# First block in a fixed program order, second norm's scale and shift moved behind the transpose, w1/w3 loaded in 4-chunk pieces

## The chip, the cores and the metric

The kernel runs on one core of a Trainium2 chip. The core has five engines that work side by side, each through its own instructions in order: PE (TensorE, matrix multiplies and transposes, writing to PSUM), DVE (VectorE, elementwise work), ACT (ScalarE, elementwise functions and PSUM copies), POOL (GpSimd) and SP (SyncE, which here issues nearly all DMA loads and stores). The metric is the device time of one execution in microseconds (us), lower is better; several runs are made and the median is given.

## What is computed

One transformer-like block over a sequence of S=2048 rows of D=576 values: a conditioned layer norm, a long convolution over the sequence, a gate, a residual, a second conditioned layer norm and a gated feed-forward layer of width F=4608. In short:

```python
sa, ca, ga, sb, cb, gb = split(silu(c) @ w_mod, 6)          # six rows of 576
h  = layernorm(x) * (1 + ca) + sa
ks = sum over t of k shifted by (3 - t) * shift_k[:, 3 - t]  # 4 taps
kv = ks * v
y  = irfft2(rfft2(kv padded) * rfft2(ssm_k padded))[:S] + kv * ssm_D
x  = x + ga * (h * y)
h  = layernorm(x) * (1 + cb) + sb
x  = x + gb * ((silu(h @ w1) * (h @ w3)) @ w2)
```

All inputs are bfloat16. w1 and w3 are 576 x 4608, w2 is 4608 x 576, w_mod is 576 x 3456.

## The kernel before

**Tiling.** The sequence is cut into 8 blocks of 256 rows and 4 rounds of 512 rows (two blocks each). The feed-forward part of a round r runs in two stages. `hidden` computes 128 columns of F at a time (a chunk; there are 36): 16 full matmuls and 2 pairs' worth of half-height ones (L512, L520) into PSUM, a Silu and a copy on ACT (L526, L528) and a product on DVE (L529) into `h3`. `down` then multiplies `h3` by w2 in 288 matmuls of 288 columns (L551); its results go through DVE (`og`, L559, L560) to the output.

**Convolution.** A block s is prepared by `kv_block` (4 taps times k, times v: eight DVE operations of 1152 elements, L252 to L258; then a forward transform on PE, L236, with PSUM copies on ACT, L239, giving `X`), `k_block` (transposes of ssm_k, L278, and a transform giving `W` and `V`), `pair` (products of one X with one V, 3456 elements each, L316, summed into `z`, L318), `gate` (layer norm of x, scaled and shifted by `arow` and `brow`) and `finish`: real parts of z (L377, L378), the inverse transform on PE (L387, 16 matmuls), times the gate (`ty`, L391) and added to x (L393), statistics on ACT (L335, L337) and POOL (L342 to L346), the second norm on DVE (L358 centers, L360 scales by the row `cbrow`, L361 shifts by `sbrow`, L417 repeats the last 64 columns), ten transposes on PE (L406) and two copies on ACT (L408) into `h2T`, which is what `hidden` of the next round reads. X and V of old blocks are stored to and read back from DRAM (`Xd`, `Vd`).

**What sets the order.** The convolution of round r+1 is written as a generator. `advance` is called after each chunk of `hidden` and each four chunks of `down` and takes as many steps out of the generator as `rate` times the cost of that piece of work allows; each `yield` says what its step cost. `rate` is the generator's total divided by a time that the round is thought to take. `end()` takes whatever is left after the last matmul of `down`. The instructions so written are then put in order on each engine by a scheduler that has its own idea of their durations. After that the order on an engine is fixed: an instruction that waits holds up all behind it on its engine, and that holds for SP's DMA issues too.

**Start.** `early_loads` issues on SP: ssm_k block 0 (`knat`), k block 0 (`kh`), v, x, and the six column groups of w_mod; on ACT's queue c, D and shift_k. shift_k is loaded to all 128 partitions at once (576 KB). `cond` makes silu(c), `mod_piece(m)` one row of 576 on all partitions with ten matmuls (L171). Round 0's `hidden` runs its first N1=20 chunks twice: once for block 0 alone (256 columns wide, while block 1's convolution, `conv_second`, is worked out), and later for block 1.

**Weights.** `load_w13` brings a piece of FC=2 chunks of w1 and w3 (four DMAs: two of 256 KB in rows of 512 B, two of 32 KB, L487, L488) into one of NW13=3 buffers `wst`. A buffer is loaded again when the matmuls that read it are done.

```python
    def advance(self, cost):
        self.due += cost
        while self.due > 0 and self.steps is not None:
            c = next(self.steps, None)
...
            self.due -= c
```

Of the kernel before, what the change touches and what calls it, by code (L numbers as in the profile page):

```python
# [10 lines left out]
F32 = mybir.dt.float32  # L11
# [14 lines left out]
FC = 2  # L26
NW13 = 3
W2C = 4
NW2 = 4
N1 = 20  # L30
# [9 lines left out]
class _Kernel:  # L40
# [28 lines left out]
    def setup(self):  # L69
# [17 lines left out]
        self.cbrow = const.tile([P, D], BF16, name="cbrow")  # L87
        self.sbrow = const.tile([P, D], BF16, name="sbrow")
# [13 lines left out]
        nc.vector.memset(self.neghalf[:], -0.5)  # L102
        nc.gpsimd.memset(self.knat[64:P, 4, :], 0.0)
        make_identity(nc, self.ident[:])

    def early_loads(self):
        nc = self.nc
        self.crow = self.hp.tile([1, D], BF16, name="crow", tag="sg")
        self.load_k(0)
        nc.scalar.dma_start(self.crow[:], self.c)  # L110
        nc.scalar.dma_start(self.drow[:], self.ssm_D.rearrange("(o d) -> o d", o=1))
        self.shk_raw = self.prod.tile([P, D, 4], BF16, name="shk_raw", tag="p")
        bap = bass.AP(tensor=self.shift_k.tensor, offset=self.shift_k.offset,
                      ap=[[0, P], [4, D], [1, 4]])
        nc.scalar.dma_start(self.shk_raw[:], bap)
# [3 lines left out]
        for m in (2, 1, 0, 4, 3, 5):  # L119
            self.load_mod(m)  # L120
# [22 lines left out]
    def shift_taps(self):  # L143
        for j in (3, 2, 1, 0):
            self.nc.vector.tensor_copy(self.shk[:, j, :], self.shk_raw[:, :, j])

    def cond(self):
# [3 lines left out]
        one = self.small.tile([1, P], BF16, name="one", tag="one", bufs=1)  # L151
        nc.vector.memset(one[:], 1.0)
# [5 lines left out]
        for ct in range(5):  # L158
            n = min(P, D - ct * P)
            nc.tensor.matmul(ptv[:n, ct * P:(ct + 1) * P], sc[0:1, ct * P:ct * P + n], one[:],  # L160
                             start=True, stop=True)
# [3 lines left out]
    def mod_piece(self, m):  # L165
# [20 lines left out]
        elif m == 4:  # L186
            nc.vector.tensor_scalar_add(two(self.cbrow), p, 1.0)
        elif m == 3:
            nc.scalar.copy(two(self.sbrow), p)
        else:  # L190
            nc.scalar.copy(two(self.gbrow), p)

# [49 lines left out]
    def kv_block(self, s):  # L242
# [16 lines left out]
        if s + 1 < NBLK:  # L259
            self.load_kv(s + 1)  # L260
        yield 0.75
        X = self.spec.tile([P, 6, D], BF16, name="X", tag="X", bufs=3)
# [6 lines left out]

    def k_block(self, s):  # L270

        nc = self.nc
# [14 lines left out]
        yield from self.forward(self.Fk, kT, lambda e, cs: W[:, 2 * e + cs, :])  # L287
        V = self.spec.tile([P, 6, D], BF16, name="V", tag="V")
# [11 lines left out]
        self.Wl[s] = W  # L300
# [48 lines left out]
    def norm(self, dst, src, mean, rstd, scale, shift):  # L349

        nc = self.nc
        n = src.shape[1]

        def row(t):
            a = t[:]
# [298 lines left out]
```

## Time and profile before

| | |
|---|---|
| runs, us | 611.83, 609.13, 607.24 (median 609.13) |
| the profiled execution, us | 607.21, of which the span of the trace is 605.4 |
| PE busy | 534.6 us (88%) |
| DVE busy | 342.7 us (57%) |
| ACT busy | 268.4 us (44%) |
| POOL busy | 45.8 us (8%) |
| DMA | 122.85 MB, 203 GB/s on average |

The span runs from the first to the last instruction of one execution. Busy shares are averages over stages of quite different kind: the first block, in which there is no feed-forward work yet; round 0, whose first half runs at half width; rounds 1 and 2, in which feed-forward and convolution run side by side; and round 3, which has no convolution left to do. A stage's length is read from the times at which PE begins the stage's first matmul.

### The profile page before, as it was taken

The page shows a single profiled execution, that of the slowest core. Times are in us where ns is not written, and L with a number is a line of the kernel's source. Part 1 is how long each engine was busy: PE and PEld are TensorE (multiplying, and loading weights), DVE is VectorE, ACT ScalarE, POOL GpSimd, SP SyncE. Part 2 cuts the span into 40 slices and gives each one's busy share as a digit, 9 for nine tenths or more (in the row PEclk, how much of TensorE's full clock was granted, in tenths as well). Part 3 has the DMA queues.
Part 4 walks back from the last instruction along what each step waited for, and adds up shares of the span by engine and source line. Part 5 has one row for each costly group of instructions (what it writes and reads, how often), then busy time and mean ns, then how long its engine had stood idle before and what let it go on. Part 6 is the DMA issues. An engine that isn't in the chain of part 4 may idle for free. (4 is left out here: it accounts for less than half of the span.)

```text
span 605.4 us, 9169 instructions
## 1 busy us (share of the span) xinstructions
PE 534.6 (88%) x3401; PEld 303.9 (50%) x3401; DVE 342.7 (57%) x543; ACT 268.4 (44%) x551; POOL 45.8 (8%) x97
## 2 busy tenths in 40 slices
PE   1748858998998889999998888999997979999996
PEld 0425534444676634444476644334475723433675
DVE  5676584847576339928885339994985131221111
ACT  3527565654423257555432256556415235545200
POOL 3112010000003103000002103000003100000000
PEclk9877997998999979999998979999998979999999
DMA  8894894989789548977796546999542535454253
GB/s 229 248 301 127 260 289 150 309 267 266 232 279 300 156 138 261 273 230 239 211 328 202 134 138 205 305 291 292 151 125 78 137 101 153 130 148 116 70 149 96
DMA packets 156370, 122.85 MB, mean 203 GB/s; under 512 B 7971, under 2 KB 147365, under 8 KB 156325
## 3 DMA queue, kind: packets, MB, share of 16 engines
q1 hardware_dynamic: 156176, 121.68, 67.5%
q10 hardware_dynamic: 148, 0.59, 0.4%
q8 instruction: 26, 0.43, 0.3%
q14 instruction: 20, 0.16, 0.1%
HBM read 108.38 MB, written 13.86 MB: 202 GB/s over the span
## 5 line engine op out<-in xcount | busy, mean ns | idle before, releaser
L512 PE MATMUL ps<-h2T,wst 128*128 128x512 bf16 (+1 forms) x1312 | 276.9, 361 | 9.2 <-DMA wst<-in_B_w_dram 6.1
L512 PEld LDWEIGHTS <-wst 128*128 128x128 bf16 x1312 | 123.6, 99 | 146.8 <-issue 37.3
L526 ACT ACTIVATE sg<-ps 128x512 bf16<-128x512 f32 (+1 forms) x164 | 89.6, 546 | 153.4 <-PE ps L520 86.9
L551 PE MATMUL ps<-w2t,h 128*128 128x288 bf16 x1152 | 149.2, 289 | 1.9 <-DMA w2t<-in_B_w_dram 1.9
L529 DVE TENSOR_TENSOR h<-sg,u 128x512 bf16<-128x512 bf16 (+1 forms) x164 | 63.7, 391 | 123.7 <-ACT u L528 123.5
L551 PEld LDWEIGHTS <-h 128*128 128x128 bf16 x1152 | 113.6, 99 | 32.0 <-DVE h2row L358 2.1
L528 ACT CAST u<-ps 128x512 bf16<-128x512 f32 (+1 forms) x164 | 87.0, 530 | 0.0
L335 ACT ACTIVATE junk<-x 128x576 bf16<-128x576 bf16 x32 | 22.0, 688 | 90.3 <-DVE x L393 80.3
L316 DVE TENSOR_TENSOR p<-X,V 128x3456 bf16<-128x3456 bf16 x28 | 54.8, 1957 | 2.6 <-DMA V<-Vd 1.7
L318 DVE TENSOR_TENSOR z<-z,p 128x3456 bf16<-128x3456 bf16 x28 | 54.8, 1957 | 0.1
L520 PE MATMUL ps<-h2T,wst 64*128 64x512 bf16 (+1 forms) x328 | 48.9, 362 | 0.9 <-DMA wst<-in_B_w_dram 0.9
L406 PE MATMUL ps<-ident,h2row 128*128 128x128 bf16 x80 | 10.7, 276 | 32.0 <-DVE h2row L361 28.7
L342 POOL TENSOR_SCALAR l2m<-l2s 128x2 f32<-128x2 f32 (+1 forms) x9 | 3.5, 387 | 378.7 <-ACT junk L335 378.7
L559 DVE TENSOR_TENSOR og<-ps,gbrow 128x288 bf16<-128x288 f32 x32 | 13.9, 454 | 30.6 <-PE ps L551 30.6
L391 DVE TENSOR_TENSOR ty<-ps,hg 128x576 bf16<-128x576 f32 x16 | 12.1, 755 | 31.5 <-PE ps L387 31.5
L520 PEld LDWEIGHTS <-wst 64*128 64x128 bf16 x328 | 10.1, 94 | 34.7 <-issue 30.5
L406 PEld LDWEIGHTS <-h2row 128*128 128x128 bf16 x80 | 6.9, 122 | 37.1 <-DVE h2row L361 31.7
L239 ACT CAST X<-ps 128x576 bf16<-128x576 f32 x32 | 19.1, 653 | 13.7 <-PE ps L236 13.7
L236 PE MATMUL ps<-kT,Fk 128*128 128x288 bf16 x128 | 18.9, 297 | 6.0 <-DVE kT L282 4.0
L337 ACT ACTIVATE junk<-x 128x576 bf16<-128x576 bf16 x32 | 22.0, 687 | 1.7
L408 ACT COPY h2T<-ps 128x640 bf16<-128x640 bf16 x16 | 11.1, 691 | 26.2 <-PE ps L406 26.2
L387 PE MATMUL ps<-z,Fb 128*128 128x288 bf16 x128 | 19.5, 303 | 3.0 <-DVE z L377 3.0
(80 smaller groups left out, 348.0 us busy)
## 6 DMA issues: line engine op xcount, KB each, us to landing
wst<-in_B_w_dram SPq DMA_DIRECT2D x164, 256.0 KB, 4.0
w2t<-in_B_w_dram SPq DMA_DIRECT2D x72, 288.0 KB, 3.0
X<-Xd SPq DMA_DIRECT2D x12, 864.0 KB, 6.0
V<-Vd SPq DMA_DIRECT2D x12, 864.0 KB, 6.7
Vd<-V SPq DMA_DIRECT2D x7, 864.0 KB, 5.3
wst<-in_B_w_dram SPq DMA_DIRECT2D x164, 32.0 KB, 4.4
Xd<-X SPq DMA_DIRECT2D x6, 864.0 KB, 5.5
kh<-in_A_k_dram SPq DMA_DIRECT2D x7, 720.0 KB, 6.3
```

The source lines that it names most:

```text
L239: nc.scalar.copy(dst(e, cs).rearrange("p (h d) -> p h d", h=2), ps[:, :, 0:H])
L316: nc.vector.tensor_mul(p[:], X[:], V[:])
L318: nc.vector.tensor_add(z[:], z[:], p[:])
L335: nc.scalar.activation(junk[:], src[:, i, :], ACT.Copy, accum_out=ssum[:, i:i + 1])
L337: nc.scalar.activation(junk[:], src[:, i, :], ACT.Square, accum_out=ssq[:, i:i + 1])
L387: nc.tensor.matmul(ps[:, h, 0:H], self.Fb[:, e, cs, cc, :], z[:, 3 * e + cs, h * H:(h + 1) * H], start=(e == 0 and cs == 1), stop=(e == 1 ...
L512: nc.tensor.matmul(gus[fi][:, i, 0:n], w[:, 5 * i + ct, fi * P:(fi + 1) * P], hT[:, ct, t0:t1], start=(first and ct == 0), stop=(not first ...
L520: nc.tensor.matmul(gus[fi][:, i, 0:n], w[rows, 4, fi * P:(fi + 1) * P], hT[rows, 4, t0:t1], start=first, stop=not first)
L526: nc.scalar.activation(sg[:, 0:n], gus[fi][:, 0, 0:n], ACT.Silu)
L528: nc.scalar.copy(u[:, 0:n], gus[fi][:, 1, 0:n])
L529: nc.vector.tensor_mul(self.h3[:, f, t0:t1], sg[:, 0:n], u[:, 0:n])
L551: nc.tensor.matmul(accs[t // 2][:, t % 2, 0:H], self.h3[:, f0 + f, t * P:(t + 1) * P], w[:, f, :], start=(f0 + f == 0), stop=(f0 + f == NF ...
```

## The change

It has five parts.

1. **First block by hand.** `first_block` writes the first block's work in one order, and `in_order` ties each PE, DVE and ACT instruction of it to the one before it on its engine. Instructions written later (block 1's) may still be put between them by the scheduler. In that order the transforms of ssm_k and of kv come ahead of all rows of w_mod, and the gate comes after the real parts of z. Fewer groups of w_mod are issued early (2, 1, 0); 4, 3 and 5 follow the load of `knat` for block 1 and precede the load of `kh` for block 1 on SP's queue.
2. **Taps.** shift_k is loaded as one row of 4.5 KB to one partition, and five PE matmuls with a row of ones spread it over the partitions; one ACT copy and two DVE copies take it from PSUM.
3. **Second norm.** The centered rows are transposed first; scale and shift are then one number per partition (`cbcol`, `sbcol`, five columns each) and applied in five ACT operations per block (alternating with DVE in block 0), in place of the two ACT copies. L360, L361 and L417 go; a second small centering of 64 columns comes. `mod_columns` computes the ten columns with 60 matmuls that have one column each. Block 0's statistics are made on DVE (`quick_stats`).
4. **Pieces.** FC=4, NW13=2: two buffers of four chunks (rows of 1 KB, DMAs of 512 KB and 64 KB); N1=24.
5. **Pace.** The steps' costs and the constants behind `rate` are new: the generator is spread over 0.86 of the round's time, not 0.93, with a total that is nearer to the sum of its steps.

```diff
-FC = 2
-NW13 = 3
+FC = 4
+NW13 = 2
...
-N1 = 20
+N1 = 24
...
     def early_loads(self):
...
-        self.load_k(0)
+        self.shk_raw = self.prod.tile([1, 4 * D], BF16, name="shk_raw", tag="p")
+        nc.scalar.dma_start(self.shk_raw[:], self.shift_k.rearrange("d j -> (d j)").rearrange("(o n) -> o n", o=1))
...
-        for m in (2, 1, 0, 4, 3, 5):
+        for m in (2, 1, 0):
             self.load_mod(m)
...
+    def mod_columns(self):
...
+        for i, m in enumerate((4, 3)):
+            for j in range(6):
...
+                for ct in range(5):
+                    nc.tensor.matmul(out, w5[:, ct, m * D + lo:m * D + lo + n], self.crep[:, ct, 0:1],
+                                     start=(ct == 0), stop=(ct == 4))
+        nc.vector.tensor_scalar_add(self.cbcol[:], ps[:, 0, 0:5], 1.0)
+        nc.vector.tensor_copy(self.sbcol[:], ps[:, 1, 0:5])
...
+    def normed(self, s, cc, m, r):
+
+        row, x1 = self.h2row, self.xo[s]
+        self.center(row[:, cc, 0:D], x1[:, cc, :], m, r)
+        self.center(row[:, cc, D:640], x1[:, cc, 512:D], m, r)
...
+                nc.scalar.activation(dst, src, ACT.Identity, bias=self.sbcol[:, ct:ct + 1],
+                                     scale=self.cbcol[:, ct:ct + 1])
...
+    def first_block(self):
...
+        self.basis(1)
+        self.shift_taps()
+        self.cond()
+        self.basis(0)
+        self.run_all(self.w_block(0))
+        self.run_all(self.kv_rows(0))
+        self.run_all(self.v_block(0))
+        self.run_all(self.x_spectrum(0))
         for m in (4, 3):
-            self.mod_piece(m)
...
+            self.load_mod(m)
+        self.load_x(1)
+        steps = self.pair(self.X[0], self.V[0], 0)
+        self.mod_piece(2)
+        self.run_all(steps)
+        self.real_parts(0)
+        self.mod_piece(1)
+        self.mod_piece(0)
+        self.run_all(self.gate(0))
+        ps = [self.inverse(0, cc) for cc in range(2)]
+        self.load_mod(5)
+        self.mod_columns()
+        more = self.kv_rows(1)
...
+        for cc in range(2):
+            self.residual(0, cc, ps[cc])
+            st.append(self.quick_stats(self.xo[0][:, cc, :], "l2"))
+        for cc in range(2):
+            self.normed(0, cc, *st[cc])
+            self.turn(pt, cc)
+            self.turned(0, pt, cc, 1, True)
...
         self.mod_piece(5)
...
+        self.in_order(since)
...
-            self.advance(rate * n / RB * 2.16)
...
+            self.advance(rate * n / RB * 2.05)
...
-            self.hidden(0, fc, 0, 256, 27.0 / (N1 * 1.08 * 0.9))
+            self.hidden(0, fc, 0, 256, 36.0 / (N1 * 1.03 * 0.8))
...
-                cost = 4 * (2 * s0 + 1) + 42
-            time = 114.0 * 0.93 - (N1 * 1.08 if r == 0 else 0)
+                cost = 8 * s0 + 50
+            time = 110.0 * 0.86 - (N1 * 1.03 if r == 0 else 0)
```

**How the order moves: PE at the end of round 0.** PE's rows in the kernel before, where the last matmuls of `down` (L551) meet the ten transposes (L406) of the second block's normed rows, `h2row`, and the first matmul of round 1's `hidden` (L512):

```order
L551 MATMUL ps<-w2t,h_102 128x288
L406 LDWEIGHTS h2row
L406 MATMUL ps<-ident,h2row 128x128
...
L512 LDWEIGHTS wst_104
L512 MATMUL ps<-h2T_107,wst_104 128x512
```

The same place after the change (L681 is `down`, L460 the transposes, L640 `hidden`):

```order
L681 MATMUL ps<-w2t,h_102 128x288
L460 LDWEIGHTS h2row
L460 MATMUL ps<-ident,h2row 128x128
...
L681 LDWEIGHTS h_102
L681 MATMUL ps<-w2t,h_102 128x288
...
L640 LDWEIGHTS wst_104
L640 MATMUL ps<-h2T_106,wst_104 128x512
```

Before, nothing of `down` stood behind the transposes. Now 98 of its 288 matmuls do, in round 1 it is 96 and in round 2 again 98. At the first half of round 0 the transposes of block 1 likewise stood behind all 20 chunks, and now nearly eight of 24 chunks stand behind them.

**DVE in the first block.** DVE's rows before, from the spectrum of block 0 (`X`) over its product (`z`), the real parts (L377, L378) and the first steps of block 1's taps (`kv`, `kvt`) to the gated result `ty`:

```order
L264 TENSOR_TENSOR X<-X 128x2x576
L187 TENSOR_SCALAR cbrow<-ps 128x576
L311 TENSOR_TENSOR z_365<-X,V 128x3456
L252 TENSOR_TENSOR kv<-kh,shk 128x1152
L377 TENSOR_TENSOR z_365<-z_365 128x2x576
L255 TENSOR_TENSOR kvt<-kh,shk 128x1152
L378 TENSOR_TENSOR z_365<-z_365 128x2x576
L256 TENSOR_TENSOR kv<-kv,kvt 128x1152
L391 TENSOR_TENSOR ty<-ps,hg 128x576
```

and after, where L278 is block 1's first tap, L354 the product, L429 and L430 the real parts, L197 and L199 `arow` and `brow`, L421 and L422 the gate and L216 the scale column from `mod_columns`:

```order
L295 TENSOR_TENSOR X<-X 128x2x576
L278 TENSOR_TENSOR kv<-kh,shk 128x1152
L354 TENSOR_TENSOR z_300<-X,V 128x3456
L281 TENSOR_TENSOR kvt<-kh,shk 128x1152
L429 TENSOR_TENSOR z_300<-z_300 128x2x576
L282 TENSOR_TENSOR kv<-kv,kvt 128x1152
L430 TENSOR_TENSOR z_300<-z_300 128x2x576
...
L199 TENSOR_TENSOR brow<-ps,ga_298 128x576
L422 TENSOR_TENSOR hg<-hg,brow 128x1152
L216 TENSOR_SCALAR cbcol<-ps 128x5
L448 TENSOR_TENSOR ty<-ps,hg 128x576
```

Block 1's first tap, which needs its own load of `kh`, now stands ahead of the product of block 0. The gate and the column from the 60 matmuls stand between the real parts and `ty`. Behind `ty` DVE has some 27 more instructions up to the last part of block 0's `h2T`, among them seven of block 1's taps and gate, and one tap of block 2 (`kh` once more) ahead of the centering of block 0.

## Rows read from the trace of the kernel before

**Rows 1.** Windows by stage: length, busy us (instructions) of each engine, granted clock, DMA.

```profile
0.00:51.23 51.23, 23.40 (x133) 15.12 (x134) 32.88 (x64) 21.78 (x42) 13.66 (x32) 0.85 0.81 242
51.23:93.89 42.66, 31.83 (x269) 22.40 (x268) 29.04 (x54) 25.94 (x68) 3.74 (x11) 0.94 0.82 242
93.89:215.38 121.49, 111.10 (x784) 69.17 (x784) 72.47 (x119) 53.31 (x118) 6.11 (x15) 0.96 0.79 241
215.38:351.34 135.96, 128.70 (x784) 69.83 (x784) 89.86 (x128) 64.38 (x126) 11.09 (x20) 0.96 0.75 225
351.34:489.99 138.65, 128.93 (x785) 70.27 (x784) 98.27 (x127) 64.37 (x126) 11.23 (x20) 0.96 0.65 190
489.99:599.70 109.71, 109.71 (x642) 56.62 (x642) 17.75 (x45) 38.64 (x72) 0.00 (x0) 0.99 0.43 121
```

**Rows 2.** Timeline of PE at two stage ends: start, us, what, [idle before it].

```profile
84.97 1.05 PE L512 MATMUL ps<-h2T,wst 128*128 128x256 bf16 x8
93.89 3.41 PE L512 MATMUL ps<-h2T,wst 128*128 128x512 bf16 x8 [0.78 <-ACT h2T L408]
...
205.10 4.08 PE L551 MATMUL ps<-w2t,h 128*128 128x288 bf16 x32
212.43 0.70 PE L406 MATMUL ps<-ident,h2row 128*128 128x128 bf16 x5 [3.25 <-DVE h2row L361]
215.38 3.57 PE L512 MATMUL ps<-h2T,wst 128*128 128x512 bf16 x8 [0.78 <-ACT h2T L408]
```

**Rows 3.** Timeline of DVE and ACT at the end of round 0.

```profile
209.69 0.77 DVE L358 TENSOR_SCALAR h2row<-x,l2m,l2r 128x576 bf16<-128x576 bf16 x2 [3.07 <-POOL l2r L346]
210.74 0.75 DVE L360 TENSOR_TENSOR h2row<-h2row,cbrow 128x1152 bf16<-128x1152 bf16 x1
213.17 0.69 ACT L408 COPY h2T<-ps 128x640 bf16<-128x640 bf16 x1 [4.87 <-PE ps L406]
```

**Rows 4.** Timeline of PE within round 2's down projection.

```profile
461.74 0.40 PE L406 MATMUL ps<-ident,h2row 128*128 128x128 bf16 x4 [3.28 <-DVE h2row L361]
```

**Rows 5.** Chain that ended last, round 3: start, us, what.

```profile
489.99 3.33 PE ps L512 x8
...
493.86 3.56 PE ps L512 x16
...
497.96 3.56 PE ps L512 x16
```

**Rows 6.** Timeline of PE, 256-wide chunks.

```profile
58.05 0.39 PE L520 MATMUL ps<-h2T,wst 64*128 64x256 bf16 x4
...
60.23 0.39 PE L520 MATMUL ps<-h2T,wst 64*128 64x256 bf16 x4
```

**Rows 7.** Timeline of the first block: PE, and an issue on SP.

```profile
19.82 0.72 PE L278 MATMUL ps<-ident,knat 128*128 128x128 bf16 x10
21.54 0.54 SPq L206 DMA_DIRECT2D kh<-in_A_k_dram  x1
35.77 3.69 PE L387 MATMUL ps<-z,Fb 128*128 128x288 bf16 x16 [3.05 <-DVE z L377]
46.96 1.65 PE L171 MATMUL ps<-h,crep 128*128 128x288 bf16 x6
```

**Rows 8.** DMA issues: KB each, median us from issue to landing.

```profile
wst<-in_B_w_dram SPq DMA_DIRECT2D x164, 256.0 KB, 4.0
kh<-in_A_k_dram SPq DMA_DIRECT2D x7, 720.0 KB, 6.3
```

**Rows 9.** Windows: the start, and the pair products of round 2 (columns as in Rows 1).

```profile
0.00:20.00 20.00, 7.04 (x39) 4.57 (x40) 10.91 (x28) 7.80 (x13) 7.65 (x17) 1.00 0.88 251
377.00:411.00 34.00, 34.00 (x167) 13.35 (x166) 33.97 (x33) 17.45 (x33) 0.00 (x0) 1.00 0.95 286
```

**Rows 10.** Groups by form: busy us, mean ns of one, idle before.

```profile
L255 DVE TENSOR_TENSOR kvt<-kh,shk 128x1152 bf16<-128x1152 bf16 x24 | 18.1, 755 | 6.4 <-DMA kh<-in_A_k_dram 6.4
L311 DVE TENSOR_TENSOR z<-X,V 128x3456 bf16<-128x3456 bf16 x8 | 15.4, 1952 | 0.0
```

More of the change, by code (lines that the diff above doesn't have):

```diff
@@ L357, in norm @@
[L357 to L368 removed]
+            return bass.AP(tensor=a.tensor, offset=a.offset, ap=[list(a.ap[0]), [0, 2], [1, D]])
@@ L369, in gate, with real_parts, inverse @@
+        nc.vector.tensor_mul(hg[:], hg[:], row(self.arow))
+        nc.vector.tensor_add(hg[:], hg[:], row(self.brow))
         self.hg[s] = hg
-        yield 2.4
-    def finish(self, s, alone):
+        yield 1.5
+    def real_parts(self, s):
         nc = self.nc
-        z = self.accs.pop(s)
-        x1 = self.xo[s]
+        z = self.accs[s]
         nc.vector.tensor_add(z[:, 1:6:3, :], z[:, 0:6:3, :], z[:, 1:6:3, :])
         nc.vector.tensor_sub(z[:, 0:6:3, :], z[:, 0:6:3, :], z[:, 2:6:3, :])
+    def inverse(self, s, cc):
+        nc = self.nc
+        z = self.accs[s]
+        ps = self.ps()
+        for cs in (1, 0):
+            for e in range(2):
+                for h in range(2):
+                    nc.tensor.matmul(ps[:, h, 0:H], self.Fb[:, e, cs, cc, :],
+                                     z[:, 3 * e + cs, h * H:(h + 1) * H],
+                                     start=(e == 0 and cs == 1), stop=(e == 1 and cs == 0))
+        return ps
@@ L398, in finish @@
-        if not alone:
-            self.norm2(s, 0, 2)
-            yield 2.4
+            ps = self.inverse(s, cc)
+            self.residual(s, cc, ps)
+            yield 1.2
+        m, r = self.ln_stats(self.xo[s], "l2")
+        yield 1.0
+        for cc in range(2):
+            self.normed(s, cc, m[:, cc:cc + 1], r[:, cc:cc + 1])
+        yield 1.0
         pt = self.ps((P, 2, 1024), BF16)
-        hT = self.h2T[(s // 2) % 2]
-        i = s % 2
         for cc in range(2):
-            for ct in range(5):
-                nc.tensor.transpose(pt[:, cc, ct * P:(ct + 1) * P], row[:, cc, ct * P:(ct + 1) * P],
-                                    self.ident[:])
-            nc.scalar.copy(hT[:, :, (2 * i + cc) * P:(2 * i + cc + 1) * P],
-                           pt[:, cc, 0:640].rearrange("p (a b) -> p a b", a=5))
@@ new lines, in finish, with run_all, in_order @@
+        self.turned(s, pt, 0, 2)
+        self.accs.pop(s)
+        self.hg.pop(s)
+        yield 0.5
+    def run_all(self, steps):
+        for _ in steps:
+            pass
+    def in_order(self, since):
+        last = {}
+        for i in self.nc.cur_bb.bb.instructions[since:]:
+            if i.engine in self.chained:
+                prev = last.get(i.engine)
+                if prev is not None:
+                    self.tc.add_manual_dep(
+                        i, prev.name,
+                        mybir.DependencyInfo(mybir.DependencyClass.NoSync, mybir.DependencyReason.DATA),
+                        reason="program order")
+                last[i.engine] = i
+        return last
@@ L506, in hidden @@
         n = t1 - t0
-        gus = [self.ps() for _ in range(FC)]
+        gus = {}
         def full(fi, first):
```

193 lines of the change are left out of this document (114 added, 79 removed).

## Prediction

> **What bounds the kernel now.** I read the windows by stage first [rows 1]. The stages are the first block (0 to 51.2), the 256-wide half of round 0 (42.7 us), the rest of round 0 (121.5), round 1 (136.0), round 2 (138.7) and round 3 (109.7). In round 3 PE is busy all the time. In rounds 1 and 2 it is busy for 129 us of 136 and 139, at a mean granted clock of 0.96, with DVE at 90 and 98 us. So PE bounds those rounds except where it stands still, and the question is where that is. In the first block PE is busy for 23 of 51 us: there the chain of loads and DVE work decides.
>
> The timeline of PE at a stage's end shows the stand-still [rows 2]. The last matmuls of round 0's `down` end at 205.10 + 4.08 = 209.2, and round 1's first matmul begins at 215.4: 6.2 us in which only ten transposes run. What PE waits for is the second norm: POOL's rstd ends at 209.7, DVE centers (0.77), scales (0.75) and shifts, and each group of transposes waits for ACT's copy of 0.69 [rows 3]. After the pause the eight matmuls take 3.57 us, where eight at speed take half of 3.56 [rows 2, 5]: the clock was at its lower level of 1.2 GHz, and that costs another 1.8 us, with the instructions behind it some 2.3. The same pause and slow start stands at the ends of rounds 1 and 2. At the end of the 256-wide half it is 93.9 − 86.0 = 7.9 us, and the start behind it loses 3.41 − 1.78 = 1.6 us. These four pauses with their slow starts come to some 35 us, and they are what the change can win.
>
> **The rounds' ends.** With 96 to 98 matmuls of `down` behind the transposes, at 4.08/32 = 0.1275 us each [rows 2], 12 us of PE work cover the copies and leave the clock up. The new norm is shorter by L360 and L361 (0.75 each, spaced 0.7) and longer by two small centerings (under 0.43 each, the price of a whole row); ACT's five operations of 256 columns lie between 5 × 0.28 (0.69 × 256/640) and 5 × 0.69 us against 2 × 0.69 before [rows 3], all under that cover. So each pause of 6.2 and each slow start goes. What comes in its place is a wait ahead of the transposes, since PE holds still there until DVE is ready. In round 2 the transposes of the first block of the pair already stand amid `down`, and PE waits 3.28 us for them [rows 4]. From the last addition to x DVE waits 3.07 us for ACT's and POOL's statistics [rows 3], and with 1.1 us of centering behind that and `ty` and x ahead (1.2) the chain from the inverse transform takes some 5.4 us; between the inverse transform and the transposes stand 28 to 56 matmuls of `down`, 3.6 to 7.1 us. Less what DVE has queued (`og` and the rest of the pairs), I expect a wait of 1 to 3 us at each of the two places per round.
>
> **Pieces.** Two chunks at full width take 497.96 − 493.86 = 4.10 us [rows 5], two at half width 60.23 − 58.05 = 2.18 [rows 6]. A piece of four is 1.18 MB. Its buffer is free when the piece is done, and it has the other piece's time to land: 8.2 us at full width, 4.36 at half. At the 285 GB/s that the start reaches at a share of 0.88 (251/0.88) [rows 9], 1.18 MB take 4.1 us, and a 256 KB load takes 4.0 us from issue to landing [rows 8], most of it not transfer (0.9 us). So a piece lands 4.1 to 7 us after its issue: in time at full width, up to 2.6 us late at half. A two-buffer cycle shares that between two pieces, so 0 to 1.3 us per piece. Some ten pieces are affected, and PE's transforms between them hide part. With three buffers of two the same bytes had two pieces to land in. I take 4 us in all for round 0 (bounds 0 and 13), and 1 to 2 us for round 2, where DMA is at a share of 0.95 while X and V stream in [rows 9]. The larger DMAs halve SP's issues for weights; what that gives lies in the same waits, so I count nothing of its own.
>
> **N1.** Four chunks more at half width in the first half cost 4 × 1.09 = +4.3; the rest of round 0 has four fewer at full width (−8.2) and four more at half (+4.3): −3.9.
>
> **First block.** It decides little of the sum but has the widest bounds. The load of shift_k (0.6 MB) goes, but `kh` of block 1 now comes behind all of ssm_k, k, v, x, w_mod and x of block 1: 6.1 MB and its own 0.74. At 285 GB/s from 2.5 us on (my choice for the first bytes) it lands at about 26; before, its issue was at 21.5 [rows 7] and typical landing 6.3 later [rows 8], with nothing waiting. Its tap stands ahead of block 0's product on DVE, whose spectrum I put at 24 (ang, taps, `crep`, `kT`, eight taps of 0.7, V and X, in that order). From 26.3: three taps, the product (1.95) and two real parts at 0.75 and less [rows 10] give 32. Before they ended at 37. The inverse transform takes 3.69 us at the lower clock [rows 7], to 35. Then PE has the 60 one-column matmuls, which no row shows. From below they cost 60 times the 0.072 us of a transpose with its weight load, 4.3 us, from above twice that, at the lower clock: 8.6 [rows 7]. I take 6, nearer the first, as the engine has been at work: `cbcol` at 41. The Trainium skill (TensorE: Matmul & The Clock Gate, Back-to-back issue gap and LDWEIGHTS) has about 81 ns for each pair of load and matmul of 128 columns, and columns/1.2 ns for a load alone: by an estimate from it 4.9 to 6.4 us, within the bounds from rows; the transposes' 72 ns here lie a little under its figure.
>
> DVE stands still at `cbcol` from 37 on, with `ty` behind it. Then come `ty` twice (1.5), x twice (0.9), four taps (2.8; one for block 2, whose `kh` can be issued only at 42 and lands at 48), four centerings (1.3 with the small ones 1.7), statistics (four operations, 0.3 to 0.43 each: 1.5), the gate of block 1 (1.5), small ones and the four `h2T` parts (1.6): 11.5 us, to 52.5. Five transposes, ACT's three parts and ten matmuls at 1.65/6 = 0.275 [rows 7], partly side by side, give 55 for the first `hidden` matmul, against 51.2: **+4**, bounds −5 and +8. Of this, block 1's taps and gate are work that the next stage no longer has to do, but that stage waits for its weights anyway.
>
> **The sum**, against the profiled execution of 607.2 (span 605.4):
> - first block +4;
> - 256-wide half: pause −7.9, chunks +4.3, a wait at block 1's transposes +2.7, late pieces +1.3: +0.4;
> - rest of round 0: chunks −3.9, slow start −1.6, pause −6.2, late pieces +2.5: −9.2;
> - round 1: −6.2 − 2.3, waits at the transposes +2: −6.5;
> - round 2: −6.2 − 2.3, waits and late pieces +3.5: −5.0;
> - round 3: slow start (3.33 against 1.78 [rows 5]): −1.6.
>
> Together −17.9: 589.3 by the profiled execution, which is 1.9 under the median of 609.13; I say **589**.
>
> **Rivals.**
> *The first block gets shorter too.* For it: z's real parts come 5 us sooner than before. If the 60 matmuls cost 4.3 and the fillers of blocks 1 and 2 are never late, `hidden` starts at 47, 8 us better than I sum, and if the waits at the transposes vanish, another 4: 577.
> *DVE is the bound, and the pause only moves into `down`.* For it: between 377 and 411 DVE is busy for all but 0.03 us of 34, in step with PE [rows 9], and PE waits 3.28 us amid `down` already [rows 4]. Against it: over the rounds DVE is busy for only 90 and 98 us of 136 and 139 [rows 1]. If half to all of the three pauses of 6.2 come back as waits, 9 to 18 us less the 6 that I have counted: 593 to 601, with a first block at its upper bound (+4) up to 605. I price it at 600.
> *Slower: two buffers starve PE.* Each piece's load starts only when its buffer is free and lands late wherever X or V (0.88 MB, 3.1 us at 285 GB/s) stands ahead of it in the queue: 4.1 + 3.1 + 2 = 9.2 us against 8.2. Some 31 pieces of rounds 0 to 2 can be hit. The kernel is slower than before once they cost 18 us more than the 6 that I count, 0.8 us each; at 1.2 us each it is 589 − 6 + 37 = 620. Against it: the windows of round 2 hold PE busy throughout at that DMA share [rows 9], and in rounds 1 and 2 the mean share is 0.75 and 0.65 [rows 1]. The Trainium skill (DMA: Bandwidth & Descriptors, Anatomy of one DMA) puts a fixed 2 us on each DMA that doesn't shrink with its size, which two deep buffers hide less well than three; by its figure the 512 KB loads would land after an estimated 3.2 us if alone, so in time at either width. The 4.0 us here for half the size show that they seldom are alone.
>
> **How the numbers follow.** My forecast's own range is 580 to 597, chance 0.54; the shorter first block 0.17 (570 to 580); DVE as bound 0.19 (597 to 608); starved by buffers 0.10 (609 to 625). A measurement of this kernel tells about 1% from no change, so faster means under 603. That takes in the first two and half of the third: 0.80; the same 0.12; slower 0.08. The range of 8 in 10 leaves out the best of the second case and most of the last: 571 to 606.
>
> **What would show it.** Right: round 1's first matmul follows `down` with no gap and at 0.22 us each; rounds 1 and 2 take 129 and 133 us; gaps ahead of L460 of 1 to 3 us; `hidden` starts near 55, DVE waits for `kh` near 24 and for PE at L216. Wrong: the first `hidden` matmul before 50 (I over-priced the columns or fillers), waits of PE for `wst` beyond 12 us in all, or gaps ahead of L460 as long as the old pauses.

## The result, and the profile after

The changed kernel takes **590.06 us** (median of 4 runs, 588.73 to 593.07) against 609.87 (607.24 to 611.83) for the kernel before, run beside it: a ratio of 0.9685, 95% interval 0.9631 to 0.9739. The profiled execution took 589.48 us with a span of 587.7. The forecast was 589.

By the windows of the same stages as in [rows 1] (length; then busy us and instructions of PE, PE's weight loads, DVE, ACT, POOL; granted clock; DMA share; GB/s) the kernel after shows:

```profile
0.00:52.35 52.35, 24.41 (x178) 15.93 (x179) 40.07 (x76) 20.60 (x37) 13.01 (x24) 0.86 0.88 271
52.35:97.00 44.65, 37.09 (x310) 26.34 (x309) 25.85 (x51) 28.68 (x78) 3.10 (x10) 0.93 0.71 232
97.00:208.86 111.86, 103.29 (x781) 68.71 (x784) 66.92 (x113) 54.14 (x126) 6.05 (x15) 0.98 0.78 249
208.86:342.39 133.53, 126.35 (x777) 69.86 (x784) 87.75 (x128) 66.01 (x132) 9.10 (x20) 0.97 0.70 228
342.39:473.90 131.51, 123.62 (x778) 68.26 (x784) 96.05 (x127) 65.97 (x132) 8.12 (x20) 1.00 0.64 201
473.90:582.00 108.10, 107.68 (x635) 56.19 (x641) 19.38 (x51) 38.64 (x72) 0.00 (x0) 1.00 0.43 125
```

Against [rows 1], stage by stage, with the forecast in brackets: first block +1.1 (+4), 256-wide half +2.0 (+0.4), rest of round 0 −9.6 (−9.2), round 1 −2.4 (−6.5), round 2 −7.1 (−5.0), round 3 −1.6 (−1.6). Together −17.7 of the span.

The ends of the rounds look as forecast. The timeline of PE at the end of round 1 and the start of round 2 (start, us, what, idle before it and what ended it):

```profile
329.80 1.00 PE L460 MATMUL ps<-ident,h2row 128*128 128x128 bf16 x10 [0.99 <-DVE h2row L406]
330.63 11.92 PE L681 MATMUL ps<-w2t,h 128*128 128x288 bf16 x96
342.39 1.89 PE L640 MATMUL ps<-h2T,wst 128*128 128x512 bf16 x7
```

The pause of 6.2 us is gone. The first eight matmuls (the record of one is missing) take 1.89 us where those of [rows 2] took 3.57; the granted clock over the first 1.8 us of this round is 1.00, over the first 3.5 us of round 1 before the change it was 0.50. So much for the picture; the experiments say that it was read wrongly.

### The profile page after: what moved, and what is told of

Read it like the earlier page. It is cut to its first block, busy times and chain, and to the rows that moved or that the text cites. A ratio compares the mean times of both kernels' runs of the same rounds, so it can differ in the third digit from the quotient of the medians.

```text
span 587.7 us, 9051 instructions
## 1 busy us (share of the span) xinstructions
PE 523.5 (89%) x3456; PEld 305.9 (52%) x3486; DVE 338.4 (58%) x547; ACT 274.0 (47%) x576; POOL 39.4 (7%) x89
## 5 line engine op out<-in xcount | busy, mean ns | idle before, releaser
L640 PE MATMUL ps<-h2T,wst 128*128 128x512 bf16 (+1 forms) x1314 | 267.7, 351 | 5.6 <-DMA wst<-in_B_w_dram 3.6
L640 PEld LDWEIGHTS <-wst 128*128 128x128 bf16 x1344 | 126.2, 99 | 134.4 <-issue 27.9
L681 PE MATMUL ps<-w2t,h 128*128 128x288 bf16 x1152 | 148.1, 289 | 0.1
L681 PEld LDWEIGHTS <-h 128*128 128x128 bf16 x1152 | 113.6, 99 | 29.8 <-issue 0.3
L361 DVE TENSOR_TENSOR z<-z,p 128x3456 bf16<-128x3456 bf16 x28 | 54.6, 1952 | 0.0
L648 PE MATMUL ps<-h2T,wst 64*128 64x512 bf16 (+1 forms) x336 | 47.1, 353 | 0.3 <-DMA wst<-in_B_w_dram 0.3
L378 ACT ACTIVATE junk<-x 128x576 bf16<-128x576 bf16 x30 | 20.6, 685 | 50.9 <-DVE x L450 50.4
L460 PE MATMUL ps<-ident,h2row 128*128 128x128 bf16 x80 | 8.9, 255 | 27.1 <-DVE h2row L406 27.0
L475 ACT ACTIVATE h2T<-ps,sbcol,cbcol 128x256 bf16<-128x256 bf16 (+1 forms) x41 | 19.4, 549 | 27.3 <-PE ps L460 25.4
L385 POOL TENSOR_SCALAR l2m<-l2s 128x2 f32<-128x2 f32 x7 | 2.3, 325 | 313.6 <-ACT junk L378 313.6
L262 PEld LDWEIGHTS <-Fk 128*128 128x128 bf16 x128 | 13.2, 104 | 19.1 <-issue 15.0
L262 PE MATMUL ps<-kv,Fb 128*128 128x288 bf16 x128 | 20.1, 306 | 2.9 <-DVE kv L284 2.1
L265 ACT CAST W<-ps 128x576 bf16<-128x576 f32 x32 | 18.7, 653 | 8.3 <-PE ps L262 8.3
L460 PEld LDWEIGHTS <-h2row 128*128 128x128 bf16 x80 | 6.2, 113 | 30.6 <-DVE h2row L406 30.1
```

Of the source, the lines that this page charges most:

```text
L262: nc.tensor.matmul(ps[:, h, 0:H], basis[:, cc, cs, e, :], rhs[:, cc, h * H:(h + 1) * H], start=(cc == 0), stop=(cc == 1))
L265: nc.scalar.copy(dst(e, cs).rearrange("p (h d) -> p h d", h=2), ps[:, :, 0:H])
L361: nc.vector.tensor_add(z[:], z[:], p[:])
L378: nc.scalar.activation(junk[:], src[:, i, :], ACT.Copy, accum_out=ssum[:, i:i + 1])
L475: nc.scalar.activation(dst, src, ACT.Identity, bias=self.sbcol[:, ct:ct + 1], scale=self.cbcol[:, ct:ct + 1])
L640: nc.tensor.matmul(gus[fi][:, i, 0:n], w[:, 5 * i + ct, fi * P:(fi + 1) * P], hT[:, ct, t0:t1], start=(first and ct == 0), stop=(not first ...
```

## The experiments

All times stand against the kernel before, which took 607.4 to 609.3 us in these runs; the intervals given are of the ratio to it. Two kernels whose ratios differ by over 0.01 are apart.

### The pace undone (e1)

```diff
-            self.advance(rate * n / RB * 2.05)
+            self.advance(rate * n / RB * 2.16)
-            self.hidden(0, fc, 0, 256, 36.0 / (N1 * 1.03 * 0.8))
+            self.hidden(0, fc, 0, 256, 27.0 / (N1 * 1.08 * 0.9))
-                cost = 8 * s0 + 50
-            time = 110.0 * 0.86 - (N1 * 1.03 if r == 0 else 0)
+                cost = 8 * s0 + 46
+            time = 114.0 * 0.93 - (N1 * 1.08 if r == 0 else 0)
```

> The changed kernel (590.1 us) with the pace constants of the kernel before; all else stays. On PE all 288 matmuls of `down` then stand ahead of the second block's transposes at the ends of rounds 0 to 2, as before the change, and in the 256-wide half the transposes stand behind 22 of 24 chunks instead of 16. Theory 1 (the gain is the earlier finish of the convolution, which keeps PE going at the upper clock over each round's end): a pause of 5 to 6 us and a start at half speed come back three times (3 x (5.5 + 2.3) = 23), less the waits amid `down` that go (some 2 a round, -6), so 604 to 611 us. Theory 2 (the second norm's scale and shift in ACT's copies, and the larger pieces, hold the gain by themselves): 590 to 597.

The steps' own costs stay those of the change.

Measured: **580.7 us**, ratio 0.9553 (0.9502 to 0.9603). The theory on which the prediction stood falls, and so does the rival: without the new pace the kernel is 9.4 us *faster* than the change. The timeline of PE at the end of round 0, with no `down` behind the transposes:

```profile
194.29 4.08 PE L681 MATMUL ps<-w2t,h 128*128 128x288 bf16 x32
199.37 1.00 PE L460 MATMUL ps<-ident,h2row 128*128 128x128 bf16 x10 [0.99 <-DVE h2row L406]
201.02 3.61 PE L640 MATMUL ps<-h2T,wst 128*128 128x512 bf16 x8 [0.66 <-ACT h2T L475]
```

With the order of before, the end of the round lasts from 198.4 to 201.0, 2.6 us, where it took 6.2 [rows 2]: the transposes come as soon as DVE has centered, and ACT's first of five parts lets `hidden` begin. The slow start is still there at the end of round 0 (3.61 us for eight, granted clock 0.52). At the ends of rounds 1 and 2 eight take 2.60 us, at a granted clock of 1.00.

What does the earlier finish cost, then? PE's groups between the first `hidden` matmul and round 3 (busy us, mean ns; idle before them and what ended it), in the changed kernel:

```profile
L262 PE MATMUL ps<-kT,Fk 128*128 128x288 bf16 x112 | 15.7, 291 | 8.4 <-ACT kT L319 8.3
L460 PE MATMUL ps<-ident,h2row 128*128 128x128 bf16 x70 | 7.5, 248 | 15.2 <-DVE h2row L406 15.1
```

and with the pace undone:

```profile
L262 PE MATMUL ps<-kT,Fk 128*128 128x288 bf16 x112 | 15.2, 285 | 2.4 <-ACT kT L319 2.3
L460 PE MATMUL ps<-ident,h2row 128*128 128x128 bf16 x70 | 6.9, 234 | 13.8 <-DVE h2row L406 13.5
```

In this stretch PE is busy for 390.4 us after the change and for 390.0 without its pace, and idle for 31.2 and 21.4: most of the loss is waits (15 of the changed kernel's 2661 matmul records are missing in this stretch, so some 3 us of its idle time may be work). 6.0 of it is the wait for ACT's copy into `kT`, 1.4 the wait for the transposes, the rest small waits and missing records. Hardly any wait at the transposes was won: an early finish only moves them to a place amid `down`.

### The new pace alone (e4)

The constants of the change, put into the kernel before (its own norm, pieces, first block, N1 and step costs); only the generator's total is 8 * s0 + 52 in place of 8 * s0 + 50.

> The kernel before (609.9 us) with the new pace alone; norm, pieces, first block and N1 are the old ones. On PE 91 to 94 matmuls of `down` then stand behind the second block's transposes in each of rounds 0 to 2. Theory 1 (the pace holds the gain): three pauses of 6.2 and slow starts of 2.3 go (-25.5), waits ahead of the transposes come, longer than with the new norm because scale and shift are still on DVE (3 to 4 us at each of two places a round, +18 to +24, less the 3.3 that stand there already), and the 256-wide half loses some of its pause of 7.9 (-5): 594 to 602. Theory 2 (without the shorter norm the pause only moves into `down`): 604 to 610. Theory 3 (the pace is all there is, the norm adds nothing): 588 to 593.

Measured: 609.62 us, ratio 1.0036 (1.0000 to 1.0073): theory 2, no gain at all. PE's groups over the same stretch:

```profile
L236 PE MATMUL ps<-kT,Fk 128*128 128x288 bf16 x112 | 16.8, 305 | 7.5 <-ACT kT L280 7.4
L406 PE MATMUL ps<-ident,h2row 128*128 128x128 bf16 x70 | 8.4, 259 | 21.6 <-DVE h2row L361 18.8 <-DVE h2row L417 2.7
```

Against the kernel before, the transposes wait 2.7 us less (24.3 there) and `hidden` no longer waits 3.1 for the copies into `h2T`; but the wait for `kT` grows by 5.5 (2.0 there), and PE stands 7.7 us for taps and copies ahead of the transform of kv, where it stood for none. The pace is no gain with either norm.

### The old norm with the old pace (e10)

```diff
-        for cc in range(2):
-            self.normed(s, cc, m[:, cc:cc + 1], r[:, cc:cc + 1])
+        for i in range(2):
+            self.center(row[:, i, 0:D], x1[:, i, :], m[:, i:i + 1], r[:, i:i + 1])
+        nc.vector.tensor_mul(row[:, :, 0:D], row[:, :, 0:D], wide(self.cbrow))
+        nc.vector.tensor_add(row[:, :, 0:D], row[:, :, 0:D], wide(self.sbrow))
+        nc.vector.tensor_copy(row[:, :, D:640], row[:, :, 512:D])
...
-        self.turned(s, pt, 0, 2)
+            nc.scalar.copy(hT[:, :, t * P:(t + 1) * P], pt[:, cc, 0:640].rearrange("p (a b) -> p a b", a=5))
```

> As e1_pace_old (580.7 us), but from block 1 on the second norm is made as before the change: DVE scales and shifts by rows of 576 (0.75 us each) and repeats the last 64 columns, ten transposes follow, then two copies on ACT of 0.69; two more rows of w_mod are made in the first block. With the pace of before, all transposes of a round's second block stand behind `down`. Theory 1, formed after e1_pace_old (the gain of the change is the shorter way from the last addition to x to `h2T`, not the pace): at the three round ends and the end of the 256-wide half the pause grows from 2.3 us (0.99 + 0.65 of waits and 0.6 of transposes) back to 6.2 to 7.9 and the start behind it is at half speed, 4 x 5 = 20 us less what a later DVE hides: 594 to 602. Theory 2 (it is the pieces and the rest, e2_pieces_old having lost 8 us): 581 to 586.

Measured: **610.62 us**, ratio 1.0043 (1.0016 to 1.0071), 30 us above the kernel that differs by the norm alone, and more than theory 1 had asked for. The end of round 0:

```profile
210.08 0.77 DVE L412 TENSOR_SCALAR h2row<-x,l2m,l2r 128x576 bf16<-128x576 bf16 x2 [1.17 <-POOL l2r L395]
210.76 0.30 DVE L710 TENSOR_TENSOR x<-x,og 128x288 bf16<-128x288 bf16 x1
210.98 0.75 DVE L502 TENSOR_TENSOR h2row<-h2row,cbrow 128x1152 bf16<-128x1152 bf16 x1
211.65 0.30 DVE L710 TENSOR_TENSOR x<-x,og 128x288 bf16<-128x288 bf16 x1
211.87 0.75 DVE L503 TENSOR_TENSOR h2row<-h2row,sbrow 128x1152 bf16<-128x1152 bf16 x1
212.67 1.25 PE L466 MATMUL ps<-ident,h2row 128*128 128x128 bf16 x10 [5.06 <-DVE h2row L503]
213.96 1.29 ACT L512 COPY h2T<-ps 128x640 bf16<-128x640 bf16 x2 [5.27 <-PE ps L466]
215.29 0.58 PE L660 MATMUL ps<-h2T,wst 128*128 128x512 bf16 x1 [1.38 <-ACT h2T L512]
216.10 2.77 PE L660 MATMUL ps<-h2T,wst 128*128 128x512 bf16 x6 [0.22 <-issue]
```

From the first centering DVE needs 2.6 us to the transposes, not 0.5, as scale, shift and two waiting operations of the output stand between; then the copies of a whole row each come ahead of the first matmul (1.38), and the six matmuls behind take 0.46 us each (the granted clock from 215.29 to 218.87 is 0.50, the lower level). From the end of `down` at 207.6 it is a pause of 7.7 us with a slow start behind it, where the kernel with the new norm has 2.6. Over the stretch as above the transposes wait 25.8 us instead of 13.8:

```profile
L466 PE MATMUL ps<-ident,h2row 128*128 128x128 bf16 x70 | 8.0, 283 | 25.8 <-DVE h2row L503 25.8
```

Not all of the 30 us is the norm: 3.9 are the first block, which makes two rows more, and with the other step costs the last inverse transform stands 16 matmuls (2 us) nearer to the end of `down` in rounds 0 to 2. Some 20 us are left for the norm by these readings, the largest gain in the change. A second comparison agrees with that size: the kernel e11 below has the old pieces and the old pace, so that it differs from the kernel before by the norm, the first block with its taps, the step costs and N1, and it is 19.5 us faster, with a first block that is 0.9 us shorter.

### The pieces (e2, e11, e6)

Three kernels. The changed kernel with the old pieces:

```diff
-FC = 4
-NW13 = 2
+FC = 2
+NW13 = 3
```

> The changed kernel with w1 and w3 in the old pieces: two chunks in each of three buffers. Theory 1 (two buffers of four cost the waits of PE for `wst` that the trace shows, 3.6 us, and of its weight loads, 4.9): these mostly go, 585 to 589 us. Theory 2 (the larger transfers win something, through half as many issues on SP's queue and rows of 1 KB): 592 to 597. If neither holds, 589 to 592.

Measured: 598.51 us, ratio 0.9845 (0.9789 to 0.9901): 8.4 us lost, on theory 2's side and beyond it. The same with the old pace:

> As e1_pace_old (580.7 us) with w1 and w3 in two chunks and three buffers, as before the change. Under the new pace this cost 8.4 us (e2_pieces_old against the changed kernel). Theory 1 (the deeper buffers gain by themselves, through waits for `wst` and for the loads behind them on SP's queue): again 586 to 591. Theory 2 (they are needed only because the faster pace bunches X, V and weights): 580 to 584.

Measured: 588.69 us, ratio 0.9664 (0.9612 to 0.9716), 8.0 above e1: theory 1. And the changed kernel with FC=2 and NW13=4, which holds the same eight chunks in smaller transfers:

> The changed kernel (590.1 us) with w1 and w3 in pieces of two chunks and four buffers: the memory of the change, the transfer size of before (256 KB in rows of 512 B). e2_pieces_old, with three such buffers, took 598.5. Theory 1 (three buffers of two hold too little ahead; the depth in bytes is what the change gained): 588 to 592. Theory 2 (the larger transfers themselves, with half as many issues and rows of 1 KB, are the gain): 596 to 600.

Measured: 590.57 us, ratio 0.9710 (0.9654 to 0.9766), the change's own time: theory 1. It is the depth in bytes that counts, eight chunks against six. Rows of 1 KB and half the issues are worth nothing that these runs show.

Where six chunks lose 8 us can be read from the stages. Nearly all of it lies in the rest of round 0, the stage with the chunks at half width: 7.2 us between e1 and e11, 8.9 between the change (111.86) and e2 (120.76). The windows of that stage in e1 and in e11, with the columns of [rows 1]:

```profile
92.84:201.02 108.18, 102.85 (x786) 68.17 (x784) 69.38 (x117) 53.17 (x127) 7.29 (x18) 1.00 0.84 267
94.30:209.71 115.41, 107.83 (x785) 69.58 (x784) 70.03 (x117) 52.96 (x125) 7.17 (x18) 0.97 0.81 245
```

2.3 us of these 7.2 are longer waits for `wst` (3.5 against 1.2); 5.0 are PE's own work, which takes longer at a mean granted clock of 0.97 against 1.00. In e2 the waits for `wst` are 5.8 us in the whole stretch (3.9 after the change), and one other wait shows what the queue does:

```profile
197.34 0.76 DVE L281 TENSOR_TENSOR kvt<-kh,shk 128x1152 bf16<-128x1152 bf16 x1 [4.08 <-DMA kh<-in_A_k_dram]
198.02 0.75 DVE L448 TENSOR_TENSOR ty<-ps,hg 128x576 bf16<-128x576 f32 x1
202.89 0.72 PE L460 MATMUL ps<-ident,h2row 128*128 128x128 bf16 x5 [4.61 <-DVE h2row L406]
```

A tap of the next block stood on DVE with its `kh` not yet there, `ty` behind it, and so the transposes waited 4.61 us where the change shows 1.49. The load had been issued among the weights at 189.22, eight us before. In e11 no such wait is seen. Which waits bring the clock down is not shown one by one.

### The chain of the first block (e3)

```diff
-        self.in_order(since)
```

The scheduler then orders the first block.

> The changed kernel without the chain that ties each instruction of the first block to the one before it on its engine: the scheduler orders them. Theory 1 (the first block gives the change nothing; it measured 52.35 us against 51.23 before): within 4 us of 590.1 either way, with the rounds behind the first block as they are. Theory 2 (the fixed order keeps the first block from being longer): 594 to 600, all of it ahead of round 0's first `hidden` matmul.

Measured: 589.59 us, ratio 0.9704 (0.9651 to 0.9758): theory 1, the fixed order is worth nothing that these runs show. `hidden` began at 50.81, and the 256-wide half behind it took 47.6 us where it takes 44.7 with the chain.

### What the new pace loses: two attempts at the copy into kT (e7, e13)

After the change PE waits for the second copy into `kT` in each round, and ACT has the gate's statistics of x (L378, L380) ahead of that copy. First only the loads of x were moved behind the second block of ssm_k in `conv`.

```diff
-        self.load_x(s0)
-        self.load_x(s1)
         X0 = self.get("X", 0)
         yield from self.k_block(s0)
         X1 = self.get("X", 1)
         yield from self.pair(X0, self.V[s0], s0)
         yield from self.k_block(s1)
+        self.load_x(s0)
+        self.load_x(s1)
```

> The changed kernel (590.1 us) with the loads of x for the next two blocks moved behind the second block's ssm_k, so that the statistics of x for the gate (L378, L380, 0.7 and 0.2 us each, eight of them) come later on ACT than the second copy into kT, which PE waits for 1.6 to 2.8 us in each round (rounds 0 to 2: 7.2 us in all). Theory 1 (these statistics ahead of the copy are the wait, and it is most of what the new pace loses against e1_pace_old): 583 to 586. Theory 2 (the wait comes from other work that the faster pace puts on ACT at that place): 588 to 592.

Measured: 589.57 us, ratio 0.9698 (0.9639 to 0.9757). This decides nothing: x landed early all the same, ACT's order was the same, and so were the waits (1.63, 2.73, 2.73 us). Then each of the statistics was tied behind the last copy into `kT` on ACT.

```diff
         m, r = self.ln_stats(x1[:], "l1")
+        for i in nc.cur_bb.bb.instructions[at:]:
+            if i.engine == nc.scalar.engine:
+                self.tc.add_manual_dep(i, self.kt_copy.name, ...)
```

> The changed kernel (590.1 us), with the statistics of x for the gate tied behind the second copy into kT on ACT (e7_late_x moved only the load of x, which landed early enough to leave ACT's order as it was). Theory 1 (those statistics are what PE's waits of 1.6 to 2.8 us for that copy are made of, and these waits are most of what the new pace loses): the waits fall by 5 us or more in all, 583 to 586. Theory 2 (the time is lost to DVE, which has fallen behind, and comes back at the next place): 588 to 592.

Measured: 588.20 us, ratio 0.9679 (0.9626 to 0.9733). The group's wait falls from 8.4 to 6.5:

```profile
L262 PE MATMUL ps<-kT,Fk 128*128 128x288 bf16 x112 | 15.4, 286 | 6.5 <-ACT kT L320 6.1 <-ACT u L665 0.4
224.00 0.65 PE L262 MATMUL ps<-kT,Fk 128*128 128x288 bf16 x4 [1.63 <-ACT kT L320]
```

1.9 us less wait there, 2.3 more for `z` at block 1's inverse transform, and 1.9 us less time, too small a step for these runs to tell from none. In rounds 1 and 2 the statistics are 1.1 of some 2.7 us; the other 1.63 stay, behind the Silu and copy of a chunk. The waits of 1.21 in the half and of 1.63 in round 0 are what they were. So theory 1 had the place right and its cause for less than half.

### A pace between, and later transposes (e12, e14)

```diff
-            time = 114.0 * 0.93 - (N1 * 1.08 if r == 0 else 0)
+            time = 114.0 * 0.90 - (N1 * 1.08 if r == 0 else 0)
```

> As e1_pace_old (580.7 us) with the generator spread over 0.90 of the round's time instead of 0.93: 32 matmuls of `down` (4.1 us) then stand behind the second block's transposes at each of the three round ends, instead of none (e1) or 96 to 98 (the change). Theory 1 (each step earlier is paid for elsewhere: rounds 0 to 2 lose time in proportion to how early the convolution is run): a little above e1, 581 to 584. Theory 2 (there is a best point between them, where the last copies are covered by 4 us of matmuls and nothing else moves): 3 x (0.65 + up to 1.7 of slow start) less than e1, 575 to 579.

Measured: 580.04 us, ratio 0.9537 (0.9482 to 0.9592), the same as e1: 32 matmuls behind the transposes neither cost nor gain. The loss sets in between there and the 96 of the change. Then the steps between the last addition to x and the transposes were made dearer, so that more of `down` stands there. With them the spread (0.86) and the rate of the half were set anew, so that 32 to 48 matmuls stay behind the last transposes and more of `hidden` stands ahead of the transposes in the half:

```diff
         m, r = self.ln_stats(self.xo[s], "l2")
-        yield 1.0
+        yield 2.5
...
             self.normed(s, cc, m[:, cc:cc + 1], r[:, cc:cc + 1])
-        yield 1.0
+        yield 1.5
...
-            self.hidden(0, fc, 0, 256, 27.0 / (N1 * 1.08 * 0.9))
+            self.hidden(0, fc, 0, 256, 33.0 / (N1 * 1.08 * 0.9))
-            time = 114.0 * 0.90 - (N1 * 1.08 if r == 0 else 0)
+            time = 114.0 * 0.86 - (N1 * 1.08 if r == 0 else 0)
```

> As e12_pace_mid (580.0 us), with larger step costs between the last addition to x and the transposes in `finish`, so that 48 matmuls of `down` (6.1 us) stand between an inverse transform and its transposes instead of 32 to 43, with a pace that leaves 32 to 48 matmuls behind the last transposes, and 40 half-width matmuls of `hidden` in place of 20 in the 256-wide half. Theory 1 (the waits ahead of the transposes, 4.07 in the half and 2.2 + 1.0 in each of rounds 0 to 2, cost what they read and only want more work in front): they fall to under 4 us in all, 570 to 575. Theory 2 (DVE is behind by then and the wait moves with the transposes): 578 to 582.

Measured: **571.92 us**, ratio 0.9417 (0.9365 to 0.9469): theory 1. Single rows of the new waits, in the half and in round 1, and the group over the stretch, first as it was in e12 and then in e14:

```profile
86.60 0.45 PE L460 MATMUL ps<-ident,h2row 128*128 128x128 bf16 x5 [1.44 <-DVE h2row L406]
297.94 1.00 PE L460 MATMUL ps<-ident,h2row 128*128 128x128 bf16 x10 [1.11 <-DVE h2row L406]
L460 PE MATMUL ps<-ident,h2row 128*128 128x128 bf16 x70 | 7.4, 247 | 13.9 <-DVE h2row L406 13.6
L460 PE MATMUL ps<-ident,h2row 128*128 128x128 bf16 x70 | 6.0, 220 | 6.3 <-DVE h2row L406 6.0
```

The wait ahead of the transposes falls from 13.9 us to 6.3, not quite to the 4 expected, and the median time by 8.1. At five of the six transposes in `down` 48 or 64 matmuls (6 us or more) now stand between the inverse transform and them, in place of 32 to 43 at five places and 53 at one (the first of round 1, where PE waited 2.35 us all the same; with 64 it waits 1.11). That the wait costs just what it reads is not shown: the profiled executions are 11.2 us apart (e12's is the slowest of its four), in the stretch PE's idle time is at most 4.9 us less, since other waits grew (the one for `kT` from 3.1 to 4.9), and its busy time at least 5.9 us less. Most of the latter is in the half, where the granted clock rose from 0.89 to 1.00 and PE's busy time fell from 38.5 us to 34.7.

### N1 undone, on the best kernel (e15)

```diff
-N1 = 24
+N1 = 20
```

> As e14_later_turns (571.9 us) with N1=20, as before the change: four chunks less at half width in the first half of round 0 (-4.3), and in the rest of the round four more at full width (+8.2) and four less at half width (-4.3), by the prediction's prices. The places of the transposes stay as in e14: 40 half-width matmuls behind the inverse transform, though 20 instead of 40 behind the transposes. Theory 1 (N1 is worth the 0.4 us that the prediction gave it): 571 to 573. Theory 2 (the four extra chunks cost their 4.3, and give nothing back): 567 to 569. Theory 3 (they are needed as cover for block 1's convolution, which is then late): 575 to 579.

Measured: 571.16 us (571.02 to 572.34), ratio 0.9382 (0.9365 to 0.9399): within theory 1's range, though 0.4 us cannot be told from nothing here. It is the fastest kernel of this study, some 18 us below the change.

## Why the number came out, and which steps were wrong

The time was hit within 1 us, but by luck and not for the reasons given: two large errors of opposite sign cancelled.

**Pieces: wrong sign.** The step "late pieces" put +6 us on the sum (bounds 0 and 13 in round 0) and no gain. The runs show −8.4 and −8.0. I compared the time in which one piece lands with the time that PE spends on the other, and found two buffers of four just short. To the kernel before I gave one sentence, "With three buffers of two the same bytes had two pieces to land in". In that measure, the time in which a piece can land, two pieces of two chunks and one of four are equal, and the runs show that the kernels are not: what differs is what is held in all, six chunks against eight. The 7.0 us of waits for `wst` before, and weights in the same queue as X, V and `kh`, were there to be read.

The rival built on the same thought, two buffers that starve PE, is out: waits for `wst` came to 3.9 us in all of PE's matmuls. The 2 us in that rival's sum of 9.2 stand on no row. By the Trainium skill (DMA: Bandwidth & Descriptors, Anatomy of one DMA — SWDGE (gpsimd) path) a part of each DMA's time does not shrink with its size; the section gives this for DMAs issued from GpSimd, while the weights here are issued from SP, and I read it against two deep buffers. The landing times agree with such a part: in the median 512 KB landed 5.1 us after the issue, and 256 KB in e6 3.9 us after it, both with what stood ahead of them in the queue. In the kernel's time it does not show: with the bytes equal, 84 loads of 512 KB and 168 of 256 KB took the same.

**The rest of the sum: too large by 15.** Without the pieces the sum was −24; the kernel that has all but the pieces (e2) is at −9. What failed is the step "With 96 to 98 matmuls of `down` behind the transposes ... So each pause of 6.2 and each slow start goes". The pauses do go, but to put the copies under 12 us of `down` gains nothing. The shorter way from x to `h2T` removes 3.6 of the 6.2 us by itself, and the early finish brings waits of its own. The pace, which I took as the means, costs 9.4 us. By medians the parts are −19.5 for the norm, the first block and N1 together (e11), −8.0 for the pieces (from e11 to e1) and +9.4 for the pace (from e1 to the change), −18.1 in all, where the change measured −19.8. No run undoes the taps or the new order of loads by themselves; the first block as a whole grew by 1.1 us.

**Waits ahead of the transposes: right.** 1 to 3 us were forecast at two places a round. They are 2.37 and 1.49, 2.67 and 0.99, 1.95 and 1.48. At block 1's transposes 4.16 came where 2.7 was summed.

**Round 1: −6.5 against −2.4.** The step lacks the wait for `kT`, 2.73, and had the waits at the transposes at 2 where they are 3.66. −8.5 + 2.73 + 3.66 gives −2.1. The work that was drawn forward put ACT, which I had looked at only behind the transposes, on PE's path: a wait at the round's start, not at its end.

**Round 2: −5.0 against −7.1.** The late pieces put in there did not come, and I had not credited that the 3.28 us amid `down` [rows 4] are among the waits replaced. With the waits at the transposes (3.43) and the one for `kT` (2.79), −8.5 + 3.43 + 2.79 − 3.28 gives −5.6; the other 1.5 are not traced.

**Rest of round 0: −9.2 against −9.6, by luck.** It is where the two errors met. With the old pieces (e2) the stage takes 120.8 us, 0.7 less than before, where the sum without its late pieces had −11.7; the pieces then gave 8.9 where +2.5 was summed. **Round 3** came as summed, −1.6. **N1**: +0.4 is not contradicted; undoing it in e15 moved the time by −0.8 us, which these runs cannot tell from none.

**First block: +4 against +1.1**, again from errors that offset one another. DVE reached the spectrum at 26.6, not at 24, `kh` of block 1 landed at 28.1, not 26, and the real parts ended at 33.5, not 32; the inverse transform was still done at 35.2, where 35 was summed. The 60 one-column matmuls cost 1.84 us where the bounds were 4.3 and 8.6. So `cbcol` was there at 38.1, three us sooner than forecast, with no wait of DVE for it. From there to the last part of `h2T` DVE took 13.8 us, not 11.5, with 2.3 us of waits for ACT's parts among them, and `hidden` began 0.4 us behind that, not 2.5: at 52.35, not 55.

**DVE as the bound** did not come: the transposes' waits in the whole stretch are 15.2 us of 421, and they fell to 6.3 once other matmuls stood ahead.

## What to carry to other kernels

When an early finish and a shorter chain are changed together, price the shorter chain first with the old order: the pause at a stage's end is the length of the chain less what covers it, and work drawn forward to hide it can queue at the stage's start, as it did on ACT here. A wait amid other work of the same engine shrinks when more of that work is put ahead of it; 6 us between a producer and its use in place of 4 to 5, in the half too, went with 8 us here. For buffers, ask of the old depth the question that is asked of the new one, and compare the bytes held in all, not numbers of buffers.

## What was not expected of the hardware

One-column matmuls with a weight load each were far cheaper than a 128-column transpose with its load (72 ns [rows 7]):

```profile
35.00 1.84 PE L214 MATMUL ps<-crep,h 128*128 128x1 bf16 x60
```

That is 31 ns each, right behind the inverse transform. The Trainium skill (TensorE: Matmul & The Clock Gate, Wait — 56ns, not 53.3ns?) states that starts are never nearer than about 25 ns however few columns there are; the row agrees. Its 81 ns for a pair of load and matmul, which I had weighed, holds for 128 columns and did not bound these.

The four operations that make `ang` took 4.04 us at the start of the kernel and 1.12 us some 9 us later:

```profile
2.04 2.98 POOL L118 MEMSET h<- 64x3456 bf16 x1
2.04 4.04 DVE L137 TENSOR_SCALAR ang<-b_row,b_col 128x256 int32<-128x256 int32 x4
11.20 1.12 DVE L137 TENSOR_SCALAR ang<-b_row,b_col 128x256 int32<-128x256 int32 x4
```

By the line's shortest, median and longest one of them took 3.13 us and the others 0.34: the group begins with POOL's memset, and the long one is about as long as that (2.98). The Trainium skill (SBUF — State Buffer, Terms) has DVE and GpSimd share one pair of ports that one instruction holds to its end, the other standing still; the row fits that. In the kernel before and in e3 all eight such operations start after that memset has ended, from 10.9 and from 6.3 us on, and each takes 0.34 to 0.36 us. No run changed this alone, and that these operations use the shared pair is not shown, so the cause is read, not shown.
